# Keys of four row tiles before their queries, with two input transposes moved ahead of the query weights

## The chip, the cores and the metric

One core of a Trainium2 chip runs the kernel. The metric is device time in microseconds (us) of one execution, lower is better; the span that the profile shows is about 1.3 us shorter than that time. Every timed comparison has runs of both kernels on the same chip. Single looks (one execution) are used for their traces only.

Names: PE is TensorE, DVE is VectorE, ACT is ScalarE, SP is SyncE, which here only issues transfers (DMAs). PEld is PE's weight load, SPq and ACTq are the sequencers of SP and ACT, where their DMAs are issued. In the profile's lines in_A_x_dram is x and in_A_wqkv_dram the weights wq, wk and wv, in the chip's memory. A DMA lands when its completion is signalled. PSUM is the memory, in banks, into which PE writes its sums and from which ACT and DVE read them.

## The reference, cut to what matters

```python
# x: 2048 x 640 bf16, cut by the kernel into 16 row tiles of 128
g = sigmoid((x * gate_w).sum(-1))
q, k, v = split(x @ wqkv)                    # 32 heads of 20
pq, pk = phi(q), phi(k)                      # phi(t) = (t + 1 if t > 0 else exp(t)) + 1e-6
num = pq @ (pk^T v);  den = pq . sum(pk)     # linear attention, per head
a = (num / den) @ wo
b = (gelu(x @ w_gate) * (x @ w_up)) @ w_down # the larger part of the work
out = g * a + (1 - g) * b
```

Only the first stage is touched by the change: pk and pq of each row tile from x, wk and wq.

## The kernel before

x is needed transposed (xT). Tiles 0 and 1 are loaded plainly (tile 0 lands 2.2 us after its issue) and transposed on PE; tiles 2 to 15 arrive by DMA transpose (3.6 us from issue to landing, the median of the fourteen). The contraction of 640 is cut into five chunks k of 128, and wk and wq arrive chunk by chunk.

```python
# loads: SP's queue and ACT's queue ("act"); a tiny load that comes first on ACT's queue is left out here
load_x(0); load_wk(0); load_x(1, "act"); load_wk(1); load_wk(3)
load_wk(2, "act"); load_wk(4, "act")
# ... gate_w on ACT's queue ...
for k in range(KC):
    load_wq(k, ("sp", "act")[k % 2])
for i in range(NXN, NT):                       # NXN = 2, NT = 16; all on SP
    load_xT(i, after=([r_wk[4]] if i == NXN else ()))
# ... then x again for the attention matrix, w_gate, w_up, wv, wo
```

The matmuls of the first stage: KM(n, [k]) and QM(n, [k]) are a pair each, 512 columns and 128 (129) columns, for one tile and one chunk. Tiles 0 and 1 do all key pairs, then all query pairs; from tile 2 on KQ(i) does keys and queries of a tile as three matmuls per chunk (512, 512 and 257 columns). phi1 is an ACT exponential, phi2 two DVE operations.

```python
warm(5, 512); warm(1, 128)                     # matmuls on constants while nothing has landed
T(0, [0], 7); T(0, [1, 2, 3, 4], 6); warm(6, 128); KM(0, [0])
T(1, [0], 7); T(1, [1, 2, 3, 4], 6); warm(3, 128); KM(1, [0])
for k in (1, 2, 3): KM(0, [k]); KM(1, [k])
gate_col(); KM(0, [4]); KM(1, [4])
for n in range(4):
    if n == 2:
        for k in range(KC): QM(2, [k]); QM(3, [k])
    phi1(n); phi2(n)
for i in range(2, NT):
    KQ(i)
# ... then MM(0): the attention matrix, whose first matmuls reuse PSUM banks 6, 7, 0 and 1
```

Of the kernel before, what the change touches and what calls it, by code (L numbers as in the profile page):

```python
# [15 lines left out]
NT = S // 128  # L16
KC = D // 128
# [4 lines left out]
XW = 656  # L22

NXN = 2


class _Res:
# [134 lines left out]
def bass_gated_mix__linear_attn_block__geglu_ffn__prompt_kernel(  # L162
# [63 lines left out]
    with (  # L226
# [8 lines left out]
        with contextlib.ExitStack() as stack:  # L235
# [12 lines left out]
            def new_dma_key():  # L248
                k = "in%d" % dma_next[0]
                dma_next[0] += 1  # L250
                return k
# [55 lines left out]
            r_xT = [P.sb("xT%d" % i, R_XT, R_XT + KC * S) for i in range(NT)]  # L307
            r_xTa = [P.sb("xTa%d" % i, R_XT, R_XT + S) for i in range(NXN)]
            r_wk = [P.sb("wk%d" % k, R_WK + k * WW, R_WK + k * WW + 640) for k in range(KC)]
# [29 lines left out]
            def dma_in(dst, src, writes, reads=(), eng="sp"):  # L339
                P.op(eng, lambda e, dst=dst, src=src: e.dma_start(dst, src),  # L340
                     reads=reads, writes=writes, dma=new_dma_key())
# [9 lines left out]
            def load_wq(k, eng="sp"):  # L351
                dma_in(wq[:, k, 0:640], A_wqkv[k * 128:(k + 1) * 128, 0:640], [r_wq[k]], eng=eng)
# [13 lines left out]
            load_wk(4, "act")  # L366
            P.op("dve", lambda e: e.memset(gw_sb, 0.0), writes=[r_gw])
            dma_in(gw_sb[0:5, :], gate_w.rearrange("(k p) -> k p", p=128), [r_gw], eng="act")
            for k in range(KC):
                load_wq(k, ("sp", "act")[k % 2])  # L370

            def load_xT(i, after=()):
                P.op("sp", lambda e: e.dma_start_transpose(xT[:, :, i * 128:(i + 1) * 128],
                                                           A_x[0, i * 128:(i + 1) * 128, :]),
                     reads=list(after), writes=[r_xT[i]], dma=new_dma_key())

            for i in range(NXN, NT):
                load_xT(i, after=([r_wk[4]] if i == NXN else ()))
            dma_in(x_aug[:, NXN:8, 0:640],
                   A_x[0, NXN * 128:8 * 128, :].rearrange("(i p) w -> p i w", p=128), r_xn[NXN:8])  # L380
            dma_in(x_aug[:, 8:NT, 0:640],
# [16 lines left out]
            def late_constants():  # L398
                P.op("pool", lambda e: e.memset(mask, 1.0), writes=[r_mask])
                for lo, hi, base, pat in ((0, 600, 0, [[0, 5], [20, 6], [0, 20]]),  # L400
                                          (600, 640, 88, [[20, 2], [0, 20]])):
                    neg = [[-s, n] for s, n in pat]
                    P.op("pool", lambda e, lo=lo, hi=hi, base=base, neg=neg: e.affine_select(
                        mask[:, lo:hi], mask[:, lo:hi], neg, ALU.is_ge, 0.0, base=-base,
                        channel_multiplier=1), reads=[r_mask], writes=[r_mask])
                    P.op("pool", lambda e, lo=lo, hi=hi, base=base, pat=pat: e.affine_select(
                        mask[:, lo:hi], mask[:, lo:hi], pat, ALU.is_ge, 0.0, base=base + 19,
                        channel_multiplier=-1), reads=[r_mask], writes=[r_mask])
# [4 lines left out]
            def warm(count, n):  # L413
                def fn(e):
                    last = None
                    for w in range(count):
                        last = e.matmul(ps[:, 4, 0:n], one_l, one_r[:, 0:n], start=True, stop=True)
                    return last
                P.op("pe", fn, writes=[bank[4]])
# [4 lines left out]
            def slot(n):  # L424
                return SLOTS[n % 4]
# [12 lines left out]
                    reads=[bank[tb]], writes=[r_xTa[i] if ks[0] == 0 else r_xT[i]])  # L438


            seq = [("k", 0), ("k", 1), ("q", 0), ("q", 1)]

            def KM(n, ks):
                i = seq[n][1]
                b0, b1 = slot(n)

                def fn(e):
                    last = None
                    for k in ks:
                        lhs = xT[:, k, i * 128:(i + 1) * 128]  # L450
                        e.matmul(ps[:, b0, :], lhs, wk[:, k, 0:512], start=(k == 0), stop=(k == KC - 1))  # L451
                        last = e.matmul(ps[:, b1, 0:128], lhs, wk[:, k, 512:640],
                                        start=(k == 0), stop=(k == KC - 1))
                    return last
                P.op("pe", fn, reads=[r_xTa[i] if i < NXN and ks == [0] else r_xT[i]] + [r_wk[k] for k in ks],
                     writes=[bank[b0], bank[b1]])

            def QM(n, ks):
                i = seq[n][1]
                b0, b1 = slot(n)  # L460

                def fn(e):
                    last = None
                    for k in ks:
                        lhs = xT[:, k, i * 128:(i + 1) * 128]
                        e.matmul(ps[:, b0, :], lhs, wq[:, k, 0:512], start=(k == 0), stop=(k == KC - 1))  # L466
                        last = e.matmul(ps[:, b1, 0:129], lhs, wq[:, k, 512:641],
                                        start=(k == 0), stop=(k == KC - 1))
                    return last
                P.op("pe", fn, reads=[r_xT[i], r_gcol] + [r_wq[k] for k in ks],  # L470
                     writes=[bank[b0], bank[b1]])

            def phi1(n):
                b0, b1 = slot(n)
                m = n % 4
                P.op("act", lambda e: e.activation(e_buf[m], ps_flat[:, b0 * 512:b0 * 512 + 640], ACT.Exp),
                     reads=[bank[b0], bank[b1]], writes=[r_e[m]])
                kind, i = seq[n]
                if kind == "q":
                    P.op("act", lambda e: e.activation(eg[:, i:i + 1], ps[:, b1, 128:129], ACT.Tanh, scale=0.5),  # L480
                         reads=[bank[b1]], writes=[r_eg[i]])

            def phi2(n):
                b0, b1 = slot(n)
                m = n % 4
                P.op("dve", lambda e: e.tensor_scalar(e_buf[m], e_buf[m], 1.0, EPS, ALU.min, ALU.add),
                     reads=[r_e[m]], writes=[r_e[m]])
                kind, i = seq[n]
                dst, r_dst = (pk[i], r_pk[i]) if kind == "k" else (pq[i], r_pq[i])
                P.op("dve", lambda e: e.scalar_tensor_tensor(  # L490
                    dst, ps_flat[:, b0 * 512:b0 * 512 + 640], 1.0 + EPS, e_buf[m], ALU.add, ALU.max),
                    reads=[bank[b0], bank[b1], r_e[m]], writes=[r_dst])
# [6 lines left out]
                     reads=[bank[7]], writes=[r_gcol])  # L499


            ALLK = list(range(KC))
            warm(5, 512)
            warm(1, 128)
            T(0, [0], 7)
# [11 lines left out]
            for k in (4,):  # L517
                KM(0, [k])
                KM(1, [k])
            for n in range(4):  # L520
                if n == 2:
                    for k in range(KC):
                        QM(2, [k])
                        QM(3, [k])
                phi1(n)
                phi2(n)

# [32 lines left out]
                phi(0, pk[i], r_pk[i], [b0, b1], ((512, 640, [b1]), (0, 512, [b0])))  # L560
                phi(1, pq[i], r_pq[i], [b1, b2], ((0, 640, [b1, b2]),))

            for i in range(2, NT):
                KQ(i)
                if i == 4:
                    late_constants()
# [359 lines left out]
```

## Time and profile before

| | |
|---|---|
| time, median of six runs | 273.89 us (273.58 to 274.39) |
| span in the profile | 272.2 us |
| PE busy | 267.9 us, 98% |
| waits of PE | 0.8 us at program start, 0.2 us once for the first wk chunk |

From the page of the kernel before, the span, the busy time by engine and the engines of the chain that ended last:

```profile
span 272.2 us, 3426 instructions
...
PE 267.9 (98%) x1343; PEld 128.1 (47%) x1369; DVE 141.8 (52%) x251; ACT 75.9 (28%) x132; POOL 30.0 (11%) x28
...
PE 95%; DVE 2%; DMA 1%; issue 1%; ACT 1%; SPq 0%; DVEq 0%; ACTq 0%
```

PE is the bound. What a change of the load order can win must therefore show as a hole in PE's work. The list of PE's waits of the kernel before (engine and line, who was waited for, total, times, longest) has almost none:

```profile
PE ps L417 <- PEq L911: 0.8, 1, 0.8
PE ps L451 <- DMA pool<-in_A_wqkv_dram: 0.2, 1, 0.2
```

PE's timeline of the kernel before (start, duration, engine, line, operation): the last warm-up group, the first key pair (L451), the second key pair of tile 0, the first query pair (L466), the first fused tile (L536):

```profile
3.55 0.62 PE L417 MATMUL ps<-const-bfloat16-1.0 128*128 128x128 bf16 x6
4.38 0.38 PE L451 MATMUL ps<-pool 128*128 128x512 bf16 x1 [0.21 <-DMA pool<-in_A_wqkv_dram]
...
5.46 0.38 PE L451 MATMUL ps<-pool 128*128 128x512 bf16 x1
...
7.67 0.38 PE L466 MATMUL ps<-pool 128*128 128x512 bf16 x1
...
10.39 29.84 PE L536 MATMUL ps<-pool 128*128 128x512 bf16 x161
```

A matmul of 512 columns shows 0.38 us because its end is modelled, but pairs follow one another every 0.27 us. From 5.46 us to 7.67 us are eight pairs and a tiny one, which is what eight pairs take: there is no hole. Read starts, not durations.

SP's queue in the kernel before, in the same columns: six loads of weights, then fourteen transposes that begin only when wk4 has landed:

```profile
1.26 2.78 SPq L340 DMA_DIRECT2D pool<-in_A_wqkv_dram  x6
...
6.51 19.01 SPq L373 DMA_TRANSPOSE pool<-in_A_x_dram  x14
```

(The x6 are wk0, wk1, wk3, wq0, wq2 and wq4: 0.46 us of issue each.)

### The profile page before, as it was taken

To read this page: it belongs to the slowest core of one execution; us is meant where nothing else is said; L and a number is where in the kernel's file an instruction comes from. 1 tells how busy PE (TensorE), PEld (TensorE's weight loads), DVE (VectorE), ACT (ScalarE), POOL (GpSimd) and SP (SyncE) were. 2 spreads that over 40 slices of the span, in tenths; PEclk is the share of its full clock that TensorE was granted. 3 is DMA by queue.
4 is the path that set the end of the run, shared out by engine and by line. 5 is a ranking of instruction groups with operands and counts; after the bars stand their busy time and mean duration, and the time that the engine had idled before them with its cause. 6 is when DMAs were issued, how large, how long until landed. Compare 5 with 4: busy or idle time off the path is not lost.

```text
span 272.2 us, 3426 instructions
## 1 busy us (share of the span) xinstructions
PE 267.9 (98%) x1343; PEld 128.1 (47%) x1369; DVE 141.8 (52%) x251; ACT 75.9 (28%) x132; POOL 30.0 (11%) x28
## 2 busy tenths in 40 slices
PE   8999999999999999999999999999999999999997
PEld 4555555544445444444444444444444444444444
DVE  2689898997333335999999999634110000000200
ACT  2555555210422453332222232224011122121021
POOL 5000000003140002242332421000000000000000
PEclk9999999999999999999999999999999999999999
DMA  6776999500300011612221221272031110110211
GB/s 219 176 114 124 349 402 384 119 2 19 61 16 2 23 50 51 200 28 48 27 48 30 43 50 25 60 229 96 5 79 37 41 39 19 39 41 19 58 58 41
DMA packets 42208, 23.61 MB, mean 87 GB/s; under 512 B 31567, under 2 KB 40783, under 8 KB 42063
## 3 DMA queue, kind: packets, MB, share of 16 engines
q1 hardware_dynamic: 41429, 22.56, 30.5%
q10 hardware_dynamic: 762, 0.82, 0.8%
q8 instruction: 11, 0.18, 0.3%
q14 instruction: 6, 0.05, 0.1%
HBM read 13.83 MB, written 2.63 MB: 60 GB/s over the span
## 4 chain that ended last, share of the span: by engine, by line
PE 95%; DVE 2%; DMA 1%; issue 1%; ACT 1%; SPq 0%; DVEq 0%; ACTq 0%
PE ps L697 41%; PE ps L861 23%; PE ps L536 12%; PE ps L593 6%; PE ps L840 4%; PE ps L808 2%; PE ps L675 2%; PE ps L596 2%; DMA pool<-in_A_wqkv_dram 1%; PE ps L451 1%; PE ps L821 1%; PE ps L466 1%; DVE pool L490 1%; PE ps L718 1%; DVE pool L555 1%
## 5 line engine op out<-in xcount | busy, mean ns | idle before, releaser
L697 PE MATMUL ps<-pool 128*128 128x512 bf16 x510 | 113.0, 379 | 0.5
L697 PEld LDWEIGHTS ps<-pool 128*128 128x128 bf16 x520 | 50.4, 98 | 60.1
L861 PE MATMUL ps<-pool 128*128 128x512 bf16 (+2 forms) x300 | 62.4, 367 | 0.3
L703 ACT ACTIVATE pool<-ps 128x512 f32<-128x512 f32 x52 | 31.0, 597 | 73.1 <-PE ps L697 73.1
L705 DVE TENSOR_TENSOR pool<-ps,pool 128x512 bf16<-128x512 f32 x52 | 34.6, 689 | 31.7 <-PE ps L697 30.4
L861 PEld LDWEIGHTS ps<-pool 128*128 128x128 bf16 x306 | 29.1, 98 | 33.5 <-issue 0.4
L536 PE MATMUL ps<-pool 128*128 128x512 bf16 (+1 forms) x206 | 37.9, 344 | 0.2
L844 DVE TENSOR_TENSOR pool<-ps,pool 128x512 bf16<-128x512 f32 x4 | 2.8, 692 | 61.5 <-PE ps L840 61.5
L751 POOL TENSOR_TENSOR pool<-pool 128x640 f32<-128x640 bf16 x16 | 22.5, 1406 | 72.8 <-DVE pool L753 65.9
L868 ACT ACTIVATE pool<-ps,pool 128x512 bf16<-128x512 f32 (+1 forms) x16 | 10.9, 680 | 68.6 <-PE ps L861 68.6
L536 PEld LDWEIGHTS ps<-pool 128*128 128x128 bf16 x210 | 20.5, 98 | 17.5
L555 DVE SCALAR_TENSOR_TENSOR pool<-ps,pool 128x128 bf16<-128x128 f32 (+2 forms) x42 | 25.3, 603 | 2.4
L546 ACT ACTIVATE pool<-ps 128x640 bf16<-128x640 f32 x28 | 19.7, 703 | 18.1 <-DVE pool L555 10.6
L593 PE MATMUL ps<-pool 128*128 128x512 bf16 x76 | 19.2, 380 | 0.1
L761 DVE TENSOR_TENSOR pool<-pool 128x640 bf16<-128x640 bf16 x16 | 13.2, 825 | 0.6
L759 DVE TENSOR_SCALAR pool<-pool 128x32 f32<-128x32 f32 x16 | 12.8, 803 | 0.6
L753 DVE TENSOR_REDUCE pool<-pool 128x32 f32<-128x640 f32 x16 | 12.9, 809 | 0.0
L641 DVE TENSOR_TENSOR pool<-pool 128x640 f32<-128x640 f32 x14 | 11.6, 826 | 0.5
L840 PE MATMUL ps<-pool 128*128 128x512 bf16 x51 | 11.5, 380 | 0.1
L643 POOL PARTITION_ALL_REDUCE pool<-pool x1 | 4.0, 3971 | 60.7 <-DVE pool L641 60.7
L593 PEld LDWEIGHTS ps<-pool 128*128 128x128 bf16 x78 | 6.9, 98 | 7.2
L552 DVE TENSOR_SCALAR pool<-pool 128x640 bf16<-128x640 bf16 x28 | 9.1, 327 | 1.8 <-ACT pool L546 0.4
(70 smaller groups left out, 105.0 us busy)
## 6 DMA issues: line engine op xcount, KB each, us to landing
out_dram<-pool SPq DMA_DIRECT2D x19, 128.0 KB, 1.7
pool<-in_B_w_gate_dram SPq DMA_DIRECT2D x1, 2080.0 KB, 14.2
pool<-in_B_w_up_dram SPq DMA_DIRECT2D x1, 2080.0 KB, 18.8
pool<-in_A_x_dram SPq DMA_DIRECT2D x1, 1280.0 KB, 8.7
pool<-in_B_w_down_dram SPq DMA_DIRECT2D x1, 1120.0 KB, 6.1
pool<-omg_row SPq DMA_DIRECT2D x1, 1024.0 KB, 4.8
pool<-in_A_wqkv_dram SPq DMA_DIRECT2D x6, 160.0 KB, 4.4
pool<-in_A_x_dram SPq DMA_DIRECT2D x1, 960.0 KB, 5.8
```

The source lines that it names most:

```text
L536: last = e.matmul(ps[:, b + p, 0:c1 - c0], xT[:, k, i * 128:(i + 1) * 128], wkq[:, k, c0:c1], start=(k == 0), stop=(k == KC - 1))
L546: P.op("act", lambda e: e.activation(e_buf[m], ps_flat[:, o:o + 640], ACT.Exp), reads=banks, writes=[r_e[m]])
L555: P.op("dve", lambda e, c0=c0, c1=c1: e.scalar_tensor_tensor(dst[:, c0:c1], ps_flat[:, o + c0:o + c1], 1.0 + EPS, e_buf[m][:, c0:c1], ALU. ...
L593: last = e.matmul(ps[:, b, :], pk[i][:, c * 128:(c + 1) * 128], x_aug[:, i, 0:512], start=(i == 0), stop=(i == NT - 1))
L697: last = e.matmul(ps[:, b, :], w[:, k, fc * 128:(fc + 1) * 128], xT[:, k, j * 512:(j + 1) * 512], start=(k == 0), stop=(k == KC - 1))
L703: P.op("act", lambda e: e.activation(ge[n], ps[:, gb, :], ACT.Gelu_apprx_tanh), reads=[bank[gb]], writes=[r_ge[n]])
L705: P.op("dve", lambda e: e.tensor_tensor(hT[fc][:, j * 512:(j + 1) * 512], ps[:, ub, :], ge[n], ALU.mult), reads=[bank[ub], r_ge[n]], write ...
L751: P.op("pool", lambda e: e.tensor_tensor(tmp[n], pq[i], z_b, ALU.mult), reads=[r_pq[i], r_zb], writes=[r_tmp[n]])
L753: P.op("dve", lambda e: e.tensor_reduce(den[n], tmp[n].rearrange("p (h d) -> p h d", h=32), AX.X, ALU.add), reads=[r_tmp[n]], writes=[r_de ...
L761: P.op("dve", lambda e: e.tensor_tensor(pq[i].rearrange("p (h d) -> p h d", h=32), pq[i].rearrange("p (h d) -> p h d", h=32), den[n].unsqu ...
L840: last = e.matmul(ps[:, b, :], wd[:, fc, 512:640], hT[fc][:, j * 512:(j + 1) * 512], start=False, stop=(fc == NFC - 2), skip_group_check=True)
L861: last = e.matmul(ps[:, pb, 0:c1 - c0], lhs, rhs, start=False, stop=(q == len(rows) - 1), skip_group_check=True)
```

## The change

The keys of tiles 0 to 3 come first, then their queries, so that wq is needed later; so the transposes of tiles 2 and 3 go onto SP's queue right behind the wk chunks, without waiting for wk4, and all of wq goes behind them on the same queue. The intent is to take wq's 0.8 MB out of the busiest time of the loads.

```diff
+NQ = 4
-            for k in range(KC):
-                load_wq(k, ("sp", "act")[k % 2])
-            for i in range(NXN, NT):
-                load_xT(i, after=([r_wk[4]] if i == NXN else ()))
+            for i in range(NXN, NQ):
+                load_xT(i)
+            for k in range(KC):
+                load_wq(k)
+            for i in range(NQ, NT):
+                load_xT(i)
...
-            seq = [("k", 0), ("k", 1), ("q", 0), ("q", 1)]
+            seq = [("k", i) for i in range(NQ)] + [("q", i) for i in range(NQ)]
...
-            for n in range(4):
-                if n == 2:
-                    for k in range(KC):
-                        QM(2, [k])
-                        QM(3, [k])
+            for n in range(2 * NQ):
+                if n in (2, 3):
+                    KM(n, ALLK)
+                if n == NQ:
+                    for k in ALLK:
+                        QM(NQ, [k])
+                        QM(NQ + 1, [k])
+                if n > NQ + 1:
+                    QM(n, ALLK)
                 phi1(n)
                 phi2(n)
...
-            for i in range(2, NT):
+            for i in range(NQ, NT):
                 KQ(i)
```

Tiles 2 and 3 thus leave the fused form and are done as key pairs and query pairs.

## The prediction

> **What bounds the kernel now.** TensorE. The page of the profile gives PE 267.9 of 272.2 us (98%), clock 9 tenths or more in all slices. The chain that ended last is 95% PE; its DMA piece is 1% (1.26 to 4.24 us, the first wk chunk). The list of PE's waits has two entries: 0.8 us at program start, 0.2 us for the first wk chunk. The timeline shows no hole in the part touched: key pairs (512 + 128 columns) follow every 0.273 us from 5.46 us; query pairs of tiles 0 and 1 run 7.67 to 10.39 us (10 pairs, 0.272 us each), fused key/query matmuls 10.39 to 48.31 us (14 tiles, 2.709 us each). The early queries do not wait for wq now: the table of windows shows DMA saturated (share 0.96 to 1.0, about 340 GB/s) from 3 to 8 us, and 1.92 MB moved by 8 us, just x tiles 0 and 1, wk and wq.
>
> **What the change moves.**
> - PE: tiles 2 and 3 go from fused (2.709 us) to pairs (5 x 2 x 0.272 = 2.72 us). Same columns, ten more weight loads (98 ns, hidden): +0.02 us.
> - DVE: two evictions cut in two (1.02 us) become whole (0.82 us), on an engine that does not bound.
> - DMA: SyncE's direct issues cost about 0.46 us each, transposes 1.28 us (the first 1.84). The first transpose drops its wait for wk4 (2.5 us, to 6.51). New order on SyncE: x0, wk0, wk1, wk3 to 2.65 us; transpose 2 to 4.5; transpose 3 to 5.8; five wq to 8.1; then transpose 4, over 1 us earlier than now (9.6). All behind is over 1 us earlier, but nothing waits for it.
>
> **Deadlines.** A transpose lands 3.6 us median after issue (2.8 to 4.2); with wk bytes ahead of it in a saturated DMA I estimate 6.5 to 7.2 us for tile 2, needed at 7.65; 7.6 to 8.5 for tile 3, needed at 9.0; wq0 8.5 to 9.5, wq4 10 to 11, needed at 10.4 and 12.5. All in time, tile 2 with the smallest margin (0.5 us). Wk chunks: the Trainium skill, "DMA: Bandwidth & Descriptors" (Queues, rings and completion order), says that each DMA engine round-robins between the queues it has work for. So wk2 and wk4 (ScalarE's queue) may share with the transpose; before they shared with wq0, as much. No run yet shows this.
> PSUM: the queries of tile 1 reuse the banks of its keys at about 10.65 us; VectorE frees them at 10.60 us now. A stall of 0 to 0.15 us.
>
> **On the critical path.** Nothing removed: the start (4.38 us) is set by x0 and wk0, whose issue is unchanged, and PE streams without holes from there. Added: 0.02 us of pairs, 0 to 0.15 us of bank wait, and with one chance in three 0.2 to 1 us for tile 2 or a late wk chunk. DMA relief may take away jitter in unprofiled runs (0.1 to 0.3 us).
>
> **Predicted:** 273.8 us, 8 in 10 between 273.2 and 274.6. Faster by over 2%: 0.01; within 2%: 0.98; slower: 0.01.
>
> **What would show it.** Right: first key matmul still at 4.4 us, fused tiles from tile 4 starting at 15.8 to 16.0 us (now tile 4 starts at 10.39 + 5.42 = 15.81), PE's list of waits under 0.5 us besides program start, transposes starting near 2.7 us and ending over 1 us earlier. Wrong: PE waiting for A_x or A_wqkv DMAs between 5 and 16 us, or the first key matmul moving.
>
> **What would make it wrong.** A transpose among plain loads slowing wk chunks more than wq did; tile 2 landing after 7.65 us; a clock loss after a stall; or queries before waiting for wq in unprofiled runs, worth up to 1 us.

## The result, and the profile after

| | before | after |
|---|---|---|
| median of six runs | 273.89 us | 274.00 us (273.77 to 274.81) |
| ratio | | 1.0007, 95% interval 0.9992 to 1.0022 |
| span in the profile | 272.2 us | 272.7 us |

A ratio is the mean time of one kernel's runs over that of the other's of the same rounds, so it is not quite the ratio of the medians quoted.

The page of the changed kernel, the same three lines:

```profile
span 272.7 us, 3467 instructions
...
PE 269.8 (99%) x1379; PEld 128.7 (47%) x1379; DVE 141.0 (52%) x249; ACT 75.9 (28%) x132; POOL 30.0 (11%) x28
...
PE 98%; DVE 1%; ACT 0%; issue 0%; DVEq 0%
```

(The busy time of PE is not comparable to a microsecond: 1343 matmuls were recorded before and 1379 after. Ten more are expected; the rest are records missing from the trace before.)

The list of PE's waits in the changed kernel is one line, so no new wait for a DMA appeared:

```profile
PE ps L419 <- PEq L917: 0.8, 1, 0.8
```

SP's queue in the changed kernel: two transposes from 2.65 us, the five wq chunks, the other twelve transposes:

```profile
2.65 2.62 SPq L371 DMA_TRANSPOSE pool<-in_A_x_dram  x2
5.32 2.48 SPq L341 DMA_DIRECT2D pool<-in_A_wqkv_dram  x5
7.84 16.50 SPq L371 DMA_TRANSPOSE pool<-in_A_x_dram  x12
```

When two of these loads landed, from the list of DMA issues in windows at 2.66 and 4.1 us (time from issue to landing last): the transposes of tiles 2 and 3, at 7.2 us (2.65 + 4.5) and 7.7 us (4.0 + 3.7):

```profile
pool<-in_A_x_dram SPq DMA_TRANSPOSE x1, 4.5
...
pool<-in_A_x_dram SPq DMA_TRANSPOSE x1, 3.7
```

PE's timeline of the changed kernel: the warm-up group, the first key pair (L453 now), the second key pair of tile 0, the first key pair of tile 2, the first query pair (L468), the first fused tile (L542):

```profile
3.55 0.85 PE L419 MATMUL ps<-const-bfloat16-1.0 128*128 128x128 bf16 x6
4.52 0.50 PE L453 MATMUL ps<-pool 128*128 128x512 bf16 x1
...
5.74 0.38 PE L453 MATMUL ps<-pool 128*128 128x512 bf16 x1
...
7.93 0.38 PE L453 MATMUL ps<-pool 128*128 128x512 bf16 x1
...
10.65 0.38 PE L468 MATMUL ps<-pool 128*128 128x512 bf16 x1
...
16.12 4.17 PE L542 MATMUL ps<-pool 128*128 128x512 bf16 x21
```

From 5.74 us on PE is as gapless as before. But this trace is 0.28 us late already at 5.74 us (5.46 before). Half of that comes from a landing: the first wk chunk landed at 4.38 us in place of 4.24, and in both traces the first key pair starts 0.14 us after that landing. The same list of issues, in a window at 1.3 us, has it, before and then after:

```profile
pool<-in_A_wqkv_dram SPq DMA_DIRECT2D x1, 160.0 KB, 3.0
...
pool<-in_A_wqkv_dram SPq DMA_DIRECT2D x1, 160.0 KB, 3.1
```

The other half comes from the clock. PE starts at half speed, and in this execution it stepped up later: the warm-up group that starts at the same 3.55 us takes 0.85 us in place of 0.62, and the first key pair still shows 0.50 us in place of 0.38. The profile's span is 0.5 us longer, and these two are 0.28 of it. Most of the rest is found at the entry of the attention matrix. The three groups there, of the kernel before (keys-times-x matmuls in banks 6 and 7, then in banks 0 and 1, then the next row tile):

```profile
48.31 0.59 PE L603 MATMUL ps<-pool 128*128 128x512 bf16 x2
48.74 0.51 PE L608 MATMUL ps<-pool 128*128 128x512 bf16 x2
49.09 0.60 PE L593 MATMUL ps<-pool 128*128 128x512 bf16 x2
```

and of the changed kernel:

```profile
48.62 0.59 PE L609 MATMUL ps<-pool 128*128 128x512 bf16 x2
49.05 0.69 PE L614 MATMUL ps<-pool 128*128 128x512 bf16 x2
49.58 0.59 PE L599 MATMUL ps<-pool 128*128 128x512 bf16 x2
```

From the first start to the third are 0.78 us before and 0.96 us after. The group in the middle takes longer: it reuses bank 1, which DVE reads for the queries of tile 14 until then (its instruction starts at 48.14 us before and at 48.63 us after, and takes 0.82 us).

So the first trace left two questions. Is the late start due to the change? And where does the 0.18 us at that entry come from?

### The profile page after: what moved, and what is told of

Its sections match the earlier page's. It is cut to its first block, busy times and chain, and to the rows that moved or that the text cites. A ratio compares the mean times of both kernels' runs of the same rounds, so it can differ in the third digit from the quotient of the medians.

```text
span 272.7 us, 3467 instructions
## 1 busy us (share of the span) xinstructions
PE 269.8 (99%) x1379; PEld 128.7 (47%) x1379; DVE 141.0 (52%) x249; ACT 75.9 (28%) x132; POOL 30.0 (11%) x28
## 4 chain that ended last, share of the span: by engine, by line
PE 98%; DVE 1%; ACT 0%; issue 0%; DVEq 0%
PE ps L703 41%; PE ps L867 23%; PE ps L542 11%; PE ps L599 6%; PE ps L846 4%; PE ps L453 2%; PE ps L468 2%; PE ps L814 2%; PE ps L681 2%; PE ps L602 1%; PE ps L419 1%; PE ps L827 1%; PE ps L724 1%; PE ps L742 0%; PE ps L469 0%; PE ps L454 0%
## 5 line engine op out<-in xcount | busy, mean ns | idle before, releaser
L703 PEld LDWEIGHTS ps<-pool 128*128 128x128 bf16 x520 | 50.5, 98 | 60.0
L867 PEld LDWEIGHTS ps<-pool 128*128 128x128 bf16 x306 | 29.2, 98 | 33.4 <-issue 0.4
L542 PE MATMUL ps<-pool 128*128 128x512 bf16 (+1 forms) x180 | 32.7, 344 | 0.0
L542 PEld LDWEIGHTS ps<-pool 128*128 128x128 bf16 x180 | 17.6, 98 | 15.0
L561 DVE SCALAR_TENSOR_TENSOR pool<-ps,pool 128x128 bf16<-128x128 f32 (+2 forms) x36 | 21.7, 603 | 2.5 <-DVE pool L558 0.5
L552 ACT ACTIVATE pool<-ps 128x640 bf16<-128x640 f32 x24 | 16.9, 703 | 16.1 <-DVE pool L561 9.0
L599 PEld LDWEIGHTS ps<-pool 128*128 128x128 bf16 x78 | 7.0, 98 | 7.2
L558 DVE TENSOR_SCALAR pool<-pool 128x640 bf16<-128x640 bf16 x24 | 7.8, 325 | 2.0 <-ACT pool L552 0.8
```

The source lines that it names most:

```text
L542: last = e.matmul(ps[:, b + p, 0:c1 - c0], xT[:, k, i * 128:(i + 1) * 128], wkq[:, k, c0:c1], start=(k == 0), stop=(k == KC - 1))
L552: P.op("act", lambda e: e.activation(e_buf[m], ps_flat[:, o:o + 640], ACT.Exp), reads=banks, writes=[r_e[m]])
L561: P.op("dve", lambda e, c0=c0, c1=c1: e.scalar_tensor_tensor(dst[:, c0:c1], ps_flat[:, o + c0:o + c1], 1.0 + EPS, e_buf[m][:, c0:c1], ALU. ...
L599: last = e.matmul(ps[:, b, :], pk[i][:, c * 128:(c + 1) * 128], x_aug[:, i, 0:512], start=(i == 0), stop=(i == NT - 1))
L703: last = e.matmul(ps[:, b, :], w[:, k, fc * 128:(fc + 1) * 128], xT[:, k, j * 512:(j + 1) * 512], start=(k == 0), stop=(k == KC - 1))
L867: last = e.matmul(ps[:, pb, 0:c1 - c0], lhs, rhs, start=False, stop=(q == len(rows) - 1), skip_group_check=True)
```

## The experiments

Two theories. **A**: the kernel before had no hole in PE's work that the change could close; both kernels are a stream of the same columns, and the rest is noise of the start. **B**: the new load order gains something at the start, and splitting tiles 2 and 3 (or something else) loses as much. Each half of the change was also run alone, because A says that each half alone must cost: wq later without needing it later, or tiles 2 and 3 earlier without having them.

To compare traces, call X the start of the second key pair of tile 0. Where that pair still ran at the half-speed clock, X is put 0.27 us before the pair that follows. A wait is measured from start to start, less the 0.27 us of a pair (the profile's own figure in brackets on a line is smaller, as it counts from the modelled end of the matmul before).

### The changed kernel again

Edit: none.

> The changed kernel once more. Theory A (nothing was on the critical path to remove, the time is TensorE's columns): ratio to before within 0.9985 to 1.0015, about 274.0 us. Theory B (the DMA order gains at the start and the split tiles lose as much): the same ratio, so this run does not tell them apart; it tightens the interval, and its trace says whether the later start seen once (keys streaming from 5.45 us in place of 5.18) belongs to the change or to the moment at which TensorE's clock steps up: if to the clock, the first key matmul and the pace of the warm-up matmuls differ from run to run of one kernel, by up to 0.3 us.

Measured: 273.98 us median, ratio 0.9987 (0.9965 to 1.0010); the kernel before had 274.38 us median on that chip, from 273.42 to 275.72. X was 6.12 us, in the same kernel that had 5.74 us in its first trace. The warm-up group and the key pairs of this run (the first of tile 0, the first of tile 1, the second of tile 0) show why:

```profile
3.55 0.84 PE L419 MATMUL ps<-const-bfloat16-1.0 128*128 128x128 bf16 x6
4.45 0.58 PE L453 MATMUL ps<-pool 128*128 128x512 bf16 x1
...
5.79 0.44 PE L453 MATMUL ps<-pool 128*128 128x512 bf16 x1
6.12 0.38 PE L453 MATMUL ps<-pool 128*128 128x512 bf16 x1
```

A matmul of 0.58 us is one at half speed, of 0.38 us one at full speed; the step falls into the pair at 5.79 us here and into the first pair at 4.52 us in the first trace. The moment of the step moves from run to run of one kernel. (The first wk chunk landed at 4.32 us here, so nearly all of the delay against 5.46 is the clock's.)

### The kernel before again

Edit: none. This is the control.

> The kernel before, once more: a control for the noise and for the clock. Call X the start of the second key pair of tile 0 (5.45 us in the first trace of before, 5.74 in the changed kernel's, 6.12 and 6.24 in two others). Theory A (the clock's step, whose moment changes from run to run, sets X): X lies anywhere from 5.45 to 6.3 us in this trace too, and span minus X is 266.7 to 267.0 us, as in all kernels that do not wait. Theory B (X is later because of the change): X is 5.45 again.

Measured: 273.72 us median, ratio to itself 0.9991 (0.9974 to 1.0009). The trace:

```profile
3.59 0.85 PE L417 MATMUL ps<-const-bfloat16-1.0 128*128 128x128 bf16 x6
4.23 0.63 PE L451 MATMUL ps<-pool 128*128 128x512 bf16 x1
...
5.68 0.38 PE L451 MATMUL ps<-pool 128*128 128x512 bf16 x1
```

X is 5.68 us, so a late start comes without the change too. Here the first wk chunk landed early, at 3.99 us, and the clock stepped late. The Trainium skill, "TensorE: Matmul & The Clock Gate" (What's actually happening), says that PE starts at half its clock and that the window which decides on the step is free-running, so that the step's moment varies with where in the window the kernel starts. These traces agree: with the same first instructions the step fell into the warm-up group at 3.55 us in the first trace of the kernel before, and behind the first key pair here; in the changed kernel it fell into the first key pair and, in its repeat, into the second. With the landing of the first wk chunk (3.99 to 4.84 us) that gave X from 5.45 to 6.51 us over all traces in the table below. Whether the change itself delays that landing by some 0.1 us is not resolved: it was at 4.23, 4.32 and 4.38 us in the first three traces with the new loads, at 3.99 to 4.24 us in the first four with the old ones, and at 4.5 us or later in all four kept traces of the last batch, with either.

### Tiles 2 and 3 as pairs, everything else as before

```diff
 # on the changed kernel: the loads of before, and
-seq = [("k", i) for i in range(NQ)] + [("q", i) for i in range(NQ)]
+seq = [(c, i) for t in (0, 2) for c in "kq" for i in (t, t + 1)]    # k0 k1 q0 q1 k2 k3 q2 q3
 # ... and the loop over n calls KM for n = 4, 5 and QM for n = 2, 3 and 6, 7
```

> The DMA order of before and its order k0 k1 q0 q1, then tiles 2 and 3 as key pairs and query pairs in place of the fused tiles: the cost of the split alone. Theory A: 10 more weight loads hide behind the matmuls, +0.02 to 0.05 us, ratio 0.9985 to 1.0015. Theory B (a gain at the start cancels the cost of the split): +0.2 to 0.4 us, ratio 1.0007 to 1.0015, and in the trace the pairs of tiles 2 and 3 take over 0.28 us each.

Measured: ratio 1.0002 (0.9979 to 1.0026). From X to the first matmul of the attention matrix it takes 42.86 us (49.33 - 6.47), against 42.85 (48.31 - 5.46) in the kernel before and 42.88 in the changed one. The split costs 0.01 to 0.04 us. The extra weight loads are hidden. B's loss is not there.

B's gain is not there either. Median times to landing, read from the list of DMA issues in short windows, are 3.0 to 4.3 us for the five wk chunks before and 3.1 to 4.3 us after. Taking wq out of their way did not make them land sooner, probably because wq was queued behind them anyway and the two transposes took its place.

### The new order of matmuls with the old loads

```diff
 # on the changed kernel
-for i in range(NXN, NQ): load_xT(i)
-for k in range(KC): load_wq(k)
-for i in range(NQ, NT): load_xT(i)
+for k in range(KC): load_wq(k, ("sp", "act")[k % 2])
+for i in range(NXN, NT): load_xT(i, after=([r_wk[4]] if i == NXN else ()))
```

> Keys of tiles 0 to 3 first, but the DMA order of before (wq on both queues, transposes behind wk4's landing). Theory A: tile 2's transpose is issued at 6.5 us, lands at about 10.2, is needed at 7.7 to 7.9: TensorE waits 2.2 to 2.6 us for A_x, and the kernel takes about 276.3 us (ratio 1.008 to 1.010). Theory B: the same wait less nothing; but if order is worth something by itself the ratio stays under 1.007.

Measured: 276.04 us median, ratio 1.0054 (1.0023 to 1.0084). The first key pairs of tiles 2 and 3 in its PE timeline:

```profile
9.39 0.39 PE L451 MATMUL ps<-pool 128*128 128x512 bf16 x1 [0.56 <-DMA pool<-in_A_x_dram]
...
11.68 0.39 PE L451 MATMUL ps<-pool 128*128 128x512 bf16 x1 [0.76 <-DMA pool<-in_A_x_dram]
```

PE waits 0.72 + 0.92 = 1.64 us for the two transposes. I had expected 2.2 to 2.6. Two inputs of that sum were off: transpose 2 landed 2.9 us after its issue (9.35 us) and not 3.7, and X was 6.47 us, a late step of the clock, so that the keys of tile 2 could not have begun before 8.67 us. With the earliest X seen, 5.45 us, the same landing times would mean an estimated wait of 1.64 + (6.47 - 5.45) = 2.66 us and the same end. A fixed landing time hides a late clock. By its ratio this run fell under the 1.007 that B named and not into A's 1.008 to 1.010. The smaller wait accounts for that, and no gain at the start shows in the trace.

### The new loads with the old order of matmuls

```diff
 # on the kernel before: its loads of wq and of xT replaced by
+for i in range(NXN, 4): load_xT(i)
+for k in range(KC): load_wq(k)
+for i in range(4, NT): load_xT(i)
```

> The DMA order of the change, but the matmul order of before (queries of tiles 0 and 1 right behind their keys). Theory A: the wq chunks land at about 8.2 to 10.8 us and are needed from 7.7 us, so TensorE waits about 0.9 us in total for A_wqkv: about 274.8 us, ratio 1.003 to 1.0045. Theory B: some of this is won back at the start, where wk chunks no longer share the DMA with wq: ratio under 1.002.

Measured: 274.63 us median, ratio 1.0013 (0.9986 to 1.0040). The time alone decides nothing here. The trace does; query pairs wait for wq twice:

```profile
8.30 0.38 PE L467 MATMUL ps<-pool 128*128 128x512 bf16 x1 [0.48 <-DMA pool<-in_A_wqkv_dram]
...
10.37 0.39 PE L467 MATMUL ps<-pool 128*128 128x512 bf16 x1 [0.28 <-DMA pool<-in_A_wqkv_dram]
```

The two waits are 0.65 + 0.44 = 1.09 us, close to the 0.9 expected, in an execution with the early clock (X 5.45). With X at 6.4 us nearly all of it would fall away, by the same reasoning as above. That would explain why the ratio lies below the expected 1.003 to 1.0045. It also met what B expected (under 1.002), but B expected it from a gain at the start, and there is none: X was 5.45 us as in the kernel before.

### Wq chunks ahead of the two early transposes

```diff
 # on the changed kernel, m = 1 or 3
+for k in range(m): load_wq(k)
 for i in range(NXN, NQ): load_xT(i)
-for k in range(KC): load_wq(k)
+for k in range(m, KC): load_wq(k)
```

> The changed kernel with one wq chunk ahead of the two early transposes. Deadline theory: tile 2's transpose is issued at 3.1 us and lands at 7.6 to 7.7; its keys can start at X + 2.20 us at the soonest. With X from 5.45 to 6.3 that is 7.65 to 8.5: no wait for A_x, or under 0.1 us. Rival (transposes among plain loads hold up the DMA, each plain load ahead costs): a wait of 0.3 us or more, or a later wk chunk.

Measured: no wait for any DMA. Transpose 2 was issued at 3.13 us and landed 4.3 us later, at 7.4 us; with X 5.82 it was needed at 8.0 us.

> The same with three wq chunks ahead: transpose 2 is issued at 4.0 us and lands at about 8.5; its keys could start at X + 2.20. Deadline theory: a wait for A_x of 8.5 - (X + 2.20): 0.85 us when the clock steps early (X 5.45), 0.1 when it steps late (X 6.2). Tile 3 and the remaining wq chunks wait for nothing. If neither kernel waits, the margin of the change is larger than I read from its trace.

Measured: two waits in the list, 0.6 us for A_x and 0.4 us for A_wqkv. The second was not foreseen: the wk chunks of this execution landed up to 5.7 us after issue, against 4.3 us in the kernel before.

> The kernel with three wq chunks ahead of the early transposes once more, because its first trace had all loads from 1.7 us on landing about 1.2 us late, with a wait of 0.4 us for a wk chunk. If that was a disturbance of that one execution, the wk chunks land 3.3 to 4.1 us after issue here, transpose 2 at about 8.5 to 9.0, and the wait for A_x is 0.2 to 1.2 us, by X. If it belongs to the order, the wk chunks are late again and the wait for A_wqkv is there again.

Measured: no wait for A_wqkv; wk chunks landed up to 4.5 us after issue, and transpose 2 at 8.8 us. The first key pair of tile 2:

```profile
8.81 0.39 PE L455 MATMUL ps<-pool 128*128 128x512 bf16 x1 [0.33 <-DMA pool<-in_A_x_dram]
```

It waits 0.49 us (the pair before started at 8.05), with X 6.12. The trace that is kept of this kernel is of another execution, with span 273.8 us: the first wk chunk landed late there, at 4.84 us, X was 6.51, transpose 2 landed at 8.94 us, and PE waited 0.28 us for it. So the deadline holds with one chunk ahead and breaks with three. The change itself has a margin of 0.8 us in its first trace (7.17 us landing, 7.93 us need) and 0.9 us in its second, where transpose 2 landed at 7.44 us. With the earliest X, 5.45 us, these landings would leave an estimated 0.5 and 0.2 us (7.65 us less the landing). Of the late wk chunks in the first look, most did not come back (up to 5.0 us after issue in the kept trace); what disturbed that execution stays open.

### The 0.2 us at the entry of the attention matrix

In the changed kernel, in both its traces, one ACT exponential of tile 14 comes late. DVE's line that releases it, and the exponential:

```profile
46.77 1.02 DVE L561 SCALAR_TENSOR_TENSOR pool<-ps,pool 128x128 bf16<-128x128 f32 x2
...
47.46 0.70 ACT L552 ACTIVATE pool<-ps 128x640 bf16<-128x640 f32 x1 [1.19 <-PE ps L542]
```

The distance between the two starts is 0.38 to 0.39 us in every other fused tile, and 0.69 us here. The note in brackets blames PE, but the matmuls of tile 14 were done at 45.9 us (one fused tile, 2.71 us, before the 48.62 above). In the kernel before the same pause of 0.3 us sits at tile 13, early enough to be partly made up. In the runs with half of the change it is not seen. A pause at a fixed place in ACT's instructions would explain that, since the change shortens ACT's stream: by the two DMA issues of wq, which "loads alone" takes off too, and by two semaphore waits, which go with the new matmuls. So instructions were put back there.

```diff
 # on the changed kernel, behind the first exponential; n = 2 or 8
+for _ in range(n):
+    P.op("act", lambda e: e.activation(eg[:, 15:16], zero, ACT.Exp), writes=[r_eg[15]])
```

> The changed kernel with two tiny activations (128 x 1) more on ScalarE while it idles at 3 to 5 us. In the changed kernel's traces one activation of tile 14 starts 0.69 us after the VectorE instruction that releases it, in place of 0.38, always at that place, and the first matmuls of the attention matrix then take 0.94 to 0.96 us in place of 0.70 to 0.79. Theory P (a pause at a fixed position in ScalarE's instruction stream, moved by the two DMA issues that the change took off that stream): with two instructions more the pause leaves that place, and the step takes about 0.70 us, as in the kernels that keep wq on ScalarE's queue. Rival (a consequence of the DMA order or of the matmul order): it stays at 0.95.

Measured: no pause in any fused tile, and the entry takes 0.70 us (lines of the kept trace, which is of another execution with the same span of 272.5 us):

```profile
48.67 0.59 PE L611 MATMUL ps<-pool 128*128 128x512 bf16 x2
49.11 0.43 PE L616 MATMUL ps<-pool 128*128 128x512 bf16 x2
49.38 0.59 PE L601 MATMUL ps<-pool 128*128 128x512 bf16 x2
```

> The same with eight tiny activations. Theory P: the pause is not at tile 14 any more, but some three tiles earlier, if it shows at all; the first matmuls of the attention matrix take 0.70 to 0.80 us. Rival: 0.95.

Measured: the pause is at tile 12, two tiles earlier than in the changed kernel. The entry still took 0.96 us: my expectation of 0.70 to 0.80 failed, as DVE had not caught up by then (its instruction for the queries of tile 14 starts at 48.65 us, as late as in the changed kernel). That the pause moves with the number of ACT instructions is shown by the two runs. The kept traces say more, if one counts the instructions that they hold for ACT, with semaphore waits and DMA issues: in all ten traces with the pause, at tile 13 (loads and matmuls of before), 14 (those of the change) or 12 (eight more), the late exponential is the 64th of them. In the other four (the three runs with half of the change, and the run with two more) the 64th is an exponential that follows on the tanh of the tile before, and no delay is seen there. So the place is fixed; what the pause is, is not shown. The Trainium skill, "Runtime: NRT & Kernel Launch" (Instruction fetch mechanics), says that instructions are refilled in blocks and that the cost of a block boundary is mostly hidden; no run here shows whether this pause is such a boundary.

### Two attempts to beat both kernels

Both use the only stretch in which PE is not streaming, the first 5.5 us. The first puts wk0 at the head of ACT's queue and uses fewer warm-up matmuls:

```diff
 # on the changed kernel
-P.op("act", ...)                 # the tiny touch load, first on ACT's queue
+load_wk(0, "act")
 load_x(0)
-load_wk(0)
 ...
-warm(6, 128)
+warm(3, 128)
 ...
-warm(3, 128); KM(1, [0]); for k in (1, 2, 3): ...
+KM(0, [1]); KM(1, [0]); KM(1, [1]); for k in (2, 3): ...
```

> An attempt to beat both: the first wk chunk goes first on ScalarE's queue (the tiny touch load dropped), six warm-up matmuls become three, and a key pair of tile 0 takes the place of the last three. If, as theory A has it, only the 5 to 6 us before the keys stream can still be shortened, the first key matmul starts at 3.9 to 4.2 us in place of 4.36 to 4.5 and the kernel gains 0.2 to 0.5 us (ratio 0.998 to 0.9993), which the interval may not resolve; the trace will. If x0 lands later because the first wk chunk shares the DMA with it, nothing is gained.

Measured: slower by a little, 274.69 us, ratio 1.0024 (1.0005 to 1.0043). The first PE transposes of tile 0:

```profile
4.00 0.72 PE L431 MATMUL ps<-pool 128*128 128x128 bf16 x5 [0.78 <-DMA pool<-in_A_x_dram]
```

They start at 4.00 us in place of 3.02 before. x0 landed 1.0 us later. That 160 KB of wk0 now moved beside it, where the tiny load had moved 0.1 KB, is the likely reason; but the edit also dropped that tiny load, and the two were not separated. PE then idled for 0.78 us, and in this trace key pairs ran at half speed until about 8.7 us.

The second leaves the loads alone, and only puts the second key pair of tile 0 in place of the last three warm-up matmuls, on the kernel before:

```diff
-warm(3, 128); KM(1, [0]); for k in (1, 2, 3): KM(0, [k]); KM(1, [k])
+KM(0, [1]); KM(1, [0]); KM(1, [1]); for k in (2, 3): KM(0, [k]); KM(1, [k])
```

> A second attempt to beat both, on the kernel before, with its loads untouched: the second key pair of tile 0 takes the place of the last three warm-up matmuls, so that TensorE does useful work while VectorE copies the transposed tile 1. wk1 lands at about 5.0 to 5.2 us, so this pair may wait 0.1 to 0.2 us. Theory A: a gain of 0 to 0.3 us, ratio 0.9988 to 1.0, below what five rounds resolve; the time from the second key pair of tile 0 to the end no longer compares, but the first fused tile starts 0 to 0.3 us sooner for the same moment of the clock's step.

Measured: 274.09 us, ratio 1.0004 (0.9988 to 1.0021). Nothing gained. The trace that is kept is of another execution than the profiled one (spans 272.7 and 272.6 us). Its first key pair, the added pair (the second of tile 0) and the first fused tile:

```profile
4.67 0.59 PE L451 MATMUL ps<-pool 128*128 128x512 bf16 x1 [0.21 <-DMA pool<-in_A_wqkv_dram]
...
5.58 0.38 PE L451 MATMUL ps<-pool 128*128 128x512 bf16 x1
...
10.93 1.24 PE L537 MATMUL ps<-pool 128*128 128x512 bf16 x5
```

The first pair waits for wk0, which landed at 4.54 us; the added pair starts 0.2 us after wk1's landing at 5.39 us. The first fused tile starts at 10.93 us, against 10.39 and 10.60 us in the two traces of the kernel before, so the 0 to 0.3 us sooner is not seen. In this trace the start followed the landings; the timed runs say that filling it differently gave nothing back.

### All traces in one sum

| kernel | X | waits for DMA after X | entry of the attention matrix | span | span less these three |
|---|---|---|---|---|---|
| before | 5.46 | 0 | 0.78 | 272.2 | 265.96 |
| before again | 5.68 | 0 | 0.79 | 272.4 | 265.93 |
| loads alone | 5.45 | 1.09 | 0.70 | 273.2 | 265.96 |
| pairs alone | 6.47 | 0 | 0.70 | 273.2 | 266.03 |
| order alone | 6.47 | 1.64 | 0.71 | 274.8 | 265.98 |
| after | 5.74 | 0 | 0.96 | 272.7 | 266.00 |
| after again | 6.12 | 0 | 0.94 | 273.1 | 266.04 |
| one wq ahead | 5.82 | 0 | 0.95 | 272.8 | 266.03 |
| three wq ahead, again | 6.12 | 0.49 | 0.94 | 273.5 | 265.95 |
| three wq ahead, again, kept trace | 6.51 | 0.28 | 0.96 | 273.8 | 266.05 |
| two ACT instructions more | 5.79 | 0 | 0.70 | 272.5 | 266.01 |
| eight ACT instructions more | 5.75 | 0 | 0.96 | 272.7 | 265.99 |

(All in us; the entry is the distance of the first to the third group of lines shown above. The first look at three wq ahead, where X itself waited for a wk chunk, and the two attempts to beat both, which change the start, are left out.) What is left is 265.93 to 266.05 us for all twelve, so three terms account for every difference between these spans to about 0.1 us. The change moves one of them, the entry, by 0.17 us. X differs by up to 1.06 us between traces, by up to 0.39 us between two of one kernel, through the clock's step and the landing of wk0.

## Why the prediction was right

It said 273.8 us, within 273.2 to 274.6; 274.00 us was measured. Point by point:

- **"Nothing removed", "PE streams without holes from there".** Right. Both kernels have the same 42.85 to 42.89 us from X to the attention matrix, and the wk chunks land within 0.2 us of where they did.
- **Pairs for fused tiles, +0.02 us.** Right: 0.01 to 0.04 us in the run with the pairs alone and in the changed kernel.
- **Deadlines.** Tile 2's transpose landed at 7.17 us (estimate 6.5 to 7.2), tile 3's at 7.74 (7.6 to 8.5), wq4 at 10.76 (10 to 11). wq0 landed at 8.26 us, sooner than the 8.5 to 9.5 said. One input was misread: the issue of 1.84 us is that of the sixth transpose of the kernel before, not of the first (1.29 us). After the change the next issue followed the first transpose 1.35 us later, so tile 3's transpose and wq0 were issued 0.5 us sooner than predicted (4.00 and 5.32 us). In the second trace of the change tile 2 landed at 7.44 us, outside the estimate. Nothing waited in either. That both halves of the change are needed together was argued, not predicted in numbers; the two runs with half of it show it, with 1.64 us and 1.09 us of waits.
- **Round robin of the queues.** The prediction expected wk2 and wk4 to suffer no more from the transpose than from wq. Their landing times agree (3.8 and 4.3 us before, 3.9 and 4.3 us after); round robin itself was not tested apart.
- **Bank wait of 0 to 0.15 us for the queries of tile 1.** 0.02 us: these pairs are 0.28 and 0.29 us apart in place of 0.27.
- **Marks.** The transposes start at 2.65 us and end at 24.3 us (25.5 before): right. The first fused tile starts at 16.12 us and not at 15.8 to 16.0, and the first key matmul at 4.52 and not 4.4: both marks failed as written, and "the first key matmul moving" was even a mark of being wrong. The prediction did say what sets that start, the landings of x0 and wk0, but took the landing of one trace for a constant: wk0 landed 0.14 us later here. The control has 4.23 us for the first key matmul and X 5.68, without any change.
- **The one chance in three of a stall, 0.2 to 1 us** did not come true; a delay that the prediction did not have, 0.17 us at the attention matrix, did. It is too small for the timed runs: their interval is 0.3% of the time, 0.8 us, wide. The number 273.8 itself is therefore partly luck in its last tenths: it counted on less jitter, which did not show, and lacked this delay.
- **Less jitter in unprofiled runs, 0.1 to 0.3 us.** Not seen: the changed kernel spread over 273.77 to 274.81 us, the kernel before over 273.58 to 274.39 us in the same rounds. In the second batch it was the other way round (273.66 to 274.67 us over six runs, against 273.42 to 275.72 us over eleven), so it stays undecided.

What stays open: what the pause on ACT is, what delayed the wk chunks in one execution, and whether the change delays the first of them by 0.1 us.

## What to carry to other kernels

Before moving loads around a tuned kernel, list the engine's starts and the landing of each load beside its deadline: where no start is late, a better load order has nothing to give, and two halves that depend on each other cost 1 to 1.6 us of waits if only one is done. Traces of short starts need a control of the unchanged kernel, because the clock's step and the landing of the first weights moved the start here by more than any edit that was free of waits. When instructions are taken off one engine, expect small shifts elsewhere: 0.2 us came from a pause that moved by one tile, because it stays at one place of the engine's instructions.

## What the Trainium skill lacked or had wrong

- "TensorE: Matmul & The Clock Gate" has the free-running window, and says that one kernel starts with more or fewer slow matmuls from run to run; these runs agree. It lacks what this does to comparing traces: here the same first instructions, with landings of the first weights that differed too, gave starts of the key stream from 5.45 to 6.51 us, 0.4% of the span and more than the effect that was sought, and a fixed landing time behind it hides the difference (1.64 us of waits with a late step).
- "DMA: Bandwidth & Descriptors" (Issuing engines are not separate DMA queues) calls the time to initiate a transfer usually small beside the transfer. Here a 160 KB load took 0.46 us of SyncE to issue and about 0.48 us to move (an estimate, 160 KB) at the 340 GB/s of that stretch, and a transpose of 160 KB took about 1.3 us to issue, so the place in the queue had much to do with the landing.
- No page that I found has a pause that sits at a fixed place of ScalarE's instructions: 0.3 us at tile 13, 14 or 12 of the loop, always before the 64th instruction that the trace holds for that engine, moved by adding two or eight instructions. "Runtime: NRT & Kernel Launch" (Instruction fetch mechanics) calls the refill of instructions mostly hidden; whether this is one is not shown.
